# Block-sparse attention with a SoLU layer: transfers of the fallback path on GpSimd, a new order of the last tiles' statistics, later key and query transposes

## The chip, the cores and the metric

The kernel runs on one core of one Trainium2 chip. The metric is the device time of one execution in microseconds. The core has five instruction streams: TensorE (PE in the profile; PEld is its weight load), VectorE (DVE), ScalarE (ACT), GpSimd (POOL) and SyncE (SP), which here issues nearly all transfers. Each stream runs in its own order and waits on semaphores.

## What is computed

Attention over 4 batches, 8 heads, 768 positions and 64 columns, with a mask on blocks of 32: the neighbours, the first and last block, and three sampled blocks per row of blocks. Then a layer on the 3072 rows of 512 values:

```python
h = x @ w_in                                    # 512 -> 1024
solu = h * softmax(h)
ln = (solu - mean(solu)) / sqrt(var(solu) + 1e-6) * g_ln
return ln @ w_out                               # 1024 -> 512
```

## The kernel before

**Units of work.** Heads are taken in pairs (4 pairs), queries in chunks of 128. A pass `ps` covers one batch and two query chunks (`PC` = 2), so there are 12 passes, 3 to a batch. In a pass each pair has 3 units (`u`), one for two chunks of keys; a unit is four score matmuls (`sco`, L416), one exp on ACT (L427) and 16 output matmuls (`op`, L444). A pass has 12 units, and a unit's number is also the clock of the plan below ("slot"). After the last unit of a pass the rows `xb` are transposed by a DMA (`x_turn`, L470, into `xT`), and the layer runs for the two tiles of 128 rows of that pass, interleaved with the next passes: `h_mms` (L487), exp (`e_exp`, L496, which also sums along the row), `solu` (L508), a DMA transpose of it (`ln_turn`, L513, into `lnT`), row statistics (`stats`, L522), `rstd` (three short instructions on DVE and a power on POOL, L540), `o_mms` (L547), scaling by rstd (`scaled`, L556 on ACT or L558 on DVE) and the store to `out` (L563).

**Keys and queries.** For batches 1 to 3 each pair's k and q are loaded by SP (`load`, L318, stage `st_k`, `st_q`), cast to bf16 on POOL into the one buffer `nat` (`cast`), and turned together by one DMA transpose that SP issues (`turn_dma`, L381, into a tile `pd` with three buffers). The transpose leaves two heads above each other on the partitions, so `shift` copies them on POOL (L327) into `KT` and `QT`, one copy a head and key, 64 partitions by 768. `KT` and `QT` have two buffers each, by the batch's parity. Pair 3 of a batch is read first by its unit 9.

**What sets the order.** Nothing is scheduled by the compiler: `at(when, fn, ...)` collects calls, and `emit` runs them sorted by `when` (in slots, a unit each), so each engine's stream has that order. The lists `first` (batch 1) and `then` (batches 2 and 3, counted from 36 slots before the batch's first unit) give the due slots of loads, casts, turns, shifts, and loads and casts of v. x's turn is due 0.1 before a pass begins (11.9, 23.9, 35.9 in that count), and a layer's ln turn at 3.05 and 9.05 of a pass. So a turn's number says behind which transposes it is on SP's queue. SP and POOL work through theirs in order: a `shift` holds POOL until its turn has landed, and a transpose that waits holds SP.

**The last tiles.** Pass 11 (`LP`) has its own tail, a list of calls that is run in its order at the end: the last h (`h_end`), exp, `solu`, statistics, transposes on PE (`ln_mm`) with a copy on ACT (`ln_out`), the output matmuls, and for the very last tile two halves (`o_half`, L893; `scale_half`, L902 on ACT and L905 on DVE), stored by SP and by ACT.

**The check and the fallback.** The fast path takes exp without the row maximum. `check_r` and `check_e` (L915, L916) mark sums out of range, `check_sum` counts them (L926, L927), `check_bad` sums over the partitions with a matmul (L932) and copies the result to `bad_i` (L933). Then every engine reads `bad_i` into a register (L985) and branches (L986): if it is over zero, `general_path` does all the work again in loops, with the maximum subtracted. With these inputs it is not, so each engine jumps over its part of `general_path` to the closing waits and barriers (L1012). What an engine has to jump over is what `general_path` puts on it; each transfer in a loop brings its address work and semaphore updates to the engine that issues it, also in the branch not taken, where the semaphores are brought to the same value.

Of the kernel before, what the change touches and what calls it, by code (L numbers as in the profile page):

```python
# [7 lines left out]
FP32 = mybir.dt.float32  # L8
# [7 lines left out]
def block_mask(nc, m_sb, m_ps, sampled_blocks, NB, neg):  # L16

    NR = sampled_blocks.shape[1]
    maskT = m_sb.tile([NB, NB], FP32, name="maskT")
    nc.vector.memset(maskT, 0.0)  # L20
    for fill, base, cm, step in (
        (neg, 1, -1, 1), (neg, 1, 1, -1),
        (0.0, -1, 1, 0), (0.0, NB - 2, -1, 0),
        (0.0, -1, 0, 1), (0.0, NB - 2, 0, -1),
    ):
        nc.gpsimd.affine_select(out=maskT, in_=maskT, compare_op=ALU.is_ge, fill=fill,
                                base=base, channel_multiplier=cm, pattern=[[step, NB]])
    _t = sampled_blocks.tensor
    _t32 = bass.DRamTensorHandle(_t.name, (2 * NB * NR,), I32)
    samp_flat_ap = bass.AP(tensor=_t32, offset=0, ap=[[0, 1], [1, 2 * NB * NR]])  # L30
    samp_i = m_sb.tile([1, NB * NR, 2], I32, name="samp_i")
    nc.sync.dma_start(out=samp_i.rearrange("a b c -> a (b c)"), in_=samp_flat_ap)
    ones1 = m_sb.tile([1, NB], BF16, name="ones1")
    nc.vector.memset(ones1, 1.0)
    samp_lo_bf = m_sb.tile([1, NB * NR], BF16, name="samp_lo_bf")
    nc.vector.tensor_copy(out=samp_lo_bf, in_=samp_i[:, :, 0])
    samp_ps = m_ps.tile([NB, NB, NR], FP32, name="samp_ps")
    nc.tensor.matmul(samp_ps.rearrange("a b c -> a (b c)"), ones1, samp_lo_bf,
                     start=True, stop=True)
    samp_f = m_sb.tile([NB, NB, NR], FP32, name="samp_f")  # L40
    nc.scalar.copy(out=samp_f, in_=samp_ps)
    kb_iota_i = m_sb.tile([NB, 1], I32, name="kb_iota_i")
    nc.gpsimd.iota(kb_iota_i, pattern=[[0, 1]], base=0, channel_multiplier=1)
    kb_iota = m_sb.tile([NB, 1], FP32, name="kb_iota")
    nc.vector.tensor_copy(out=kb_iota, in_=kb_iota_i)
    eq = m_sb.tile([NB, NB, NR], FP32, name="eq")
    nc.vector.tensor_scalar(out=eq, in0=samp_f, scalar1=kb_iota, scalar2=None, op0=ALU.is_equal)
    anyeq = m_sb.tile([NB, NB], FP32, name="anyeq")
    nc.vector.reduce_sum(out=anyeq, in_=eq, axis=AX.X)
    nc.vector.tensor_scalar(out=anyeq, in0=anyeq, scalar1=-1.0, scalar2=1.0,  # L50
                            op0=ALU.mult, op1=ALU.add)
    nc.vector.tensor_scalar(out=anyeq, in0=anyeq, scalar1=0.0, scalar2=None, op0=ALU.max)
    nc.vector.tensor_mul(out=maskT, in0=maskT, in1=anyeq)
    return maskT


def general_path(tc, q, k, v, sampled_blocks, w_in_sb, w_out_sb, ident, out):
# [10 lines left out]
    with tc.tile_pool(name="f_c", bufs=1) as f_c, \  # L68
# [5 lines left out]
        with tc.tile_pool(name="f_m", bufs=1) as f_m, \  # L74
             tc.tile_pool(name="f_mp", bufs=1, space=bass.MemoryType.PSUM) as f_mp:
            maskT = block_mask(nc, f_m, f_mp, sampled_blocks, NB, -1e30)
            sel = f_m.tile([NB, NB, BLK], FP32, name="sel")
            nc.vector.memset(sel, 0.0)
            nc.gpsimd.affine_select(out=sel, in_=sel, compare_op=ALU.not_equal, fill=1.0,
                                    base=0, channel_multiplier=1, pattern=[[-1, NB], [0, BLK]])  # L80
            for t in (qT, kT):
                nc.vector.memset(t[D:TQ, :], 0.0)
            nc.vector.tensor_copy(out=kT[D : D + NB, :].rearrange("p (q o) -> p q o", o=BLK),
                                  in_=sel)
            m_row = f_m.tile([NB, NB, BLK], BF16, name="m_row")
            nc.vector.tensor_copy(
                out=m_row,
                in_=maskT.rearrange("p (q o) -> p q o", o=1).broadcast_to([NB, NB, BLK]))
            nc.sync.dma_start(out=m_scr, in_=m_row.rearrange("p q o -> p (q o)"))
        with tc.tile_pool(name="f_sb", bufs=2) as f_sb, \  # L90
             tc.tile_pool(name="f_ps", bufs=1, space=bass.MemoryType.PSUM) as f_ps:
            with tc.For_i(0, B, 1) as b:
                with tc.For_i(0, H, 1) as h:
# [11 lines left out]
                    with tc.For_i(0, S, TQ) as t0:  # L105
# [1 line left out]
                        nc.gpsimd.dma_start(  # L107
                            out=qc, in_=q[bass.ds(b, 1), bass.ds(h, 1), bass.ds(t0, TQ), :].rearrange(
                                "a e p d -> p (a e d)"))
                        nc.sync.dma_start(out=qT[D : D + NB, :], in_=m_scr[:, bass.ds(t0, TQ)])  # L110
                        tq = f_ps.tile([D, TQ], BF16, tag="f_tq")
                        nc.tensor.matmul(tq, qc, ident, is_transpose=True, start=True, stop=True)
                        nc.vector.tensor_copy(out=qT[0:D, :], in_=tq)
# [22 lines left out]
                        for j in range(NCH):  # L136
# [4 lines left out]
                        xo = f_sb.tile([TQ, D], BF16, tag="f_x")  # L141
                        nc.vector.tensor_scalar(out=xo, in0=op, scalar1=rs, scalar2=None,
                                                op0=ALU.mult)
                        nc.sync.dma_start(
                            out=x_scr[bass.ds(b, 1), bass.ds(t0, TQ), bass.ds(h * D, D)].rearrange(
                                "a p d -> p (a d)"),
                            in_=xo)
# [1 line left out]
        with tc.tile_pool(name="f_sb2", bufs=2) as f_sb, \  # L149
             tc.tile_pool(name="f_ps2", bufs=1, space=bass.MemoryType.PSUM) as f_ps:  # L150
            with tc.For_i(0, n_tok, 128) as t0:
                xt = f_sb.tile([128, d_model], BF16, tag="f_xt")
                nc.sync.dma_start(out=xt, in_=x_rows[bass.ds(t0, 128), :])
                tps = f_ps.tile([128, KD, 128], BF16, tag="f_tps")
                for c in range(KD):
                    nc.tensor.matmul(tps[:, c, :], xt[:, c * 128 : (c + 1) * 128], ident,
# [45 lines left out]
                                     stop=(c == KF - 1))  # L202
                ot = f_sb.tile([128, d_model], FP32, tag="f_ot")
                nc.scalar.copy(out=ot, in_=ops)
                nc.sync.dma_start(out=out[bass.ds(t0, 128), :], in_=ot)


@with_exitstack
def kernel(
# [80 lines left out]
    def at(when, fn, *args):  # L290
        plan.append((when, len(plan), fn, args))
# [31 lines left out]
    def copy(eng, o, i):  # L323
        if eng is nc.scalar:
            nc.scalar.copy(out=o, in_=i)
        else:
            eng.tensor_copy(out=o, in_=i)  # L327
# [52 lines left out]
        turned[b, pr] = pt  # L380
        nc.sync.dma_start_transpose(out=pt, in_=nat[:, 2 * PW * pr : 2 * PW * (pr + 1)])  # L381

    def shift(b, pr, key):
        n0 = NCH if key == "q" else 0
        dst = (KT if key == "k" else QT)[b % 2]
        for hh in range(2):
            h = 2 * pr + hh
            copy(nc.gpsimd, dst[0:D, h * NCH : (h + 1) * NCH, :],
                 turned[b, pr][hh * D : (hh + 1) * D, n0 : n0 + NCH, :])

# [181 lines left out]
    with tc.manual_schedule():  # L574
# [195 lines left out]
        for s in range(n_units):  # L770
# [19 lines left out]
            [21.3, 21.4, 26.0, 27.3, 30.1, 30.15, 38.2, 39.0],  # L790
            [9.7, 27.08, 27.3, 36.2], [18.0, 30.07, 32.0, 41.0])
        then = (
            [3.2, 4.1, 5.0, 5.9, 15.2, 16.1, 17.9, 18.3], [8.2, 9.4, 10.6, 11.8, 20.2, 21.4, 23.8, 24.5],
            [13.0, 21.1, 25.0, 27.1],
            [15.4, 16.4, 24.03, 24.9, 27.4, 28.4, 30.6, 31.5],
            [17.0, 28.1, 29.0, 37.05], [22.6, 33.4, 34.6, 41.0])
        for b in range(1, B):
            loads, casts, turns, shifts, v_loads, v_casts = first if b == 1 else then
            t0 = SLOTS * NPB * (b - 1)
            for (key, pr), t_l, t_c in zip(kq + vs, loads + v_loads, casts + v_casts):  # L800
                at(t0 + t_l, load, nc.sync, srcs[key], b, pr, key)
                at(t0 + t_c, cast, nc.gpsimd, b, pr, key)
            for pr, t_t in enumerate(turns):
                at(t0 + t_t, turn_dma, b, pr)
            for (key, pr), t_s in zip(kq, shifts):
                at(t0 + t_s, shift, b, pr, key)


        def layer(ps, i, hs, es, os):
# [74 lines left out]

        o2 = {}

        def o_half(half, pool, tag):
            if pool is p_sco:
                o2[half] = p_sco.tile([128, 2, HF], FP32, tag=tag, name="oe1a")[:, 0, 0:256]
            else:  # L890
                o2[half] = pool.tile([128, d_model], FP32, tag=tag, name="oe1b")[:, 0:256]
            for c in range(KF):
                nc.tensor.matmul(o2[half], lnT_of[LP, 1][:, c, :],  # L893
                                 w_cen_sb[:, c, half * 256 : (half + 1) * 256],
                                 start=(c == 0), stop=(c == KF - 1), skip_group_check=True)
# [29 lines left out]
        def check_sum():  # L925
            nc.vector.reduce_sum(out=n_ok[:, 0:1], in_=okr, axis=AX.X)  # L926
            nc.vector.tensor_scalar(out=bad, in0=n_ok[:, 0:1], scalar1=float(n_r + n_e),  # L927
                                    scalar2=None, op0=ALU.is_lt)

        def check_bad():  # L930
            bad_ps = p_h.tile([1, 1], FP32, tag="h", name="bad_ps")
            nc.tensor.matmul(bad_ps, bad, ones_c, start=True, stop=True)  # L932
            nc.vector.tensor_copy(out=bad_i, in_=bad_ps)  # L933

        end = SLOTS * NPASS
        A, V = nc.scalar, nc.vector
        for n, (fn, *args) in enumerate((
# [7 lines left out]
            (check_r, n_r - 2 * PC, n_r),  # L945
            (h_end, 1, 0, KD),
            (solu, LP, 0),
            (e_exp, LP, 1),
            (o_mms, LP - 1, 1, 0, 3, tile_in(p_op, "op", "o_10")),
            (ln_mm, 0),  # L950
            (ln_out, 0, A),
            (o_mms, LP - 1, 1, 3, 8),
            (solu, LP, 1),
            (check_e,),
            (stats, LP, 0),
            (rstd, LP, 0),
            (o_mms, LP, 0, 0, 2, tile_in(p_sco, "sco", "oe0")),
            (ln_mm, 1),
            (ln_out, 1, A),
            (stats, LP, 1),  # L960
            (rstd, LP, 1),
            (o_mms, LP, 0, 2, 8),
            (scaled, LP - 1, 1, A),
            (store, LP - 1, 1),
            (check_sum,),
            (scaled, LP, 0, A),
            (store, LP, 0),
            (o_half, 0, p_sco, "sco"),
            (o_half, 1, p_op, "op"),
            (scale_half, 0, V, nc.sync),  # L970
            (scale_half, 1, A, nc.scalar),
            (check_bad,),
        )):
            at(end + 0.01 * n, fn, *args)
        at(end - 5.0, x_turn, LP, 0, 2)
# [41 lines left out]
```

## Time and profile before

| | us |
|---|---|
| median of 3 runs | 213.96 (213.76 to 214.35) |
| the profiled execution | 213.1 |
| its span, first to last instruction | 211.5 |
| mean granted TensorE clock | 0.989 |

The span is shorter than the execution's time by 1.6 us, which lies before the first and after the last instruction. In rows of the profile "out<-in" names tiles of the program with their numbers left out, "x4" is the number of instructions in the row, "idle before" or the bracket says how long the engine stood idle and who ended it. A busy time of merged rows runs from the first start to the last end, so neighbours overlap.

### The profile page before, as it was taken

Reading aid. Unit: us, or ns where it says so; the run is one execution under the profiler, and the core shown is the slowest. Engines: PE = TensorE matmul, PEld = TensorE weight load, DVE = VectorE, ACT = ScalarE, POOL = GpSimd, SP = SyncE. Lnnn points to the kernel's source line nnn. Section 1 sums busy time; section 2 is a strip of 40 time slices with the busy share of each in tenths; the row PEclk is TensorE's granted clock in tenths of the full one; section 3 lists DMA queues with packets and bytes.
Section 4 is the critical chain, followed back from the end, with each engine's and each line's share of the span. In section 5 each row is a group of like instructions: output and inputs, shape, how many; then the busy total and the mean of one; then the engine's idle time right before and its main releaser. Section 6 shows DMA issues by size and latency. Waiting matters only on the chain.

```text
span 211.5 us, 5629 instructions
## 1 busy us (share of the span) xinstructions
PE 199.9 (95%) x2238; PEld 137.5 (65%) x2238; DVE 139.9 (66%) x329; ACT 174.5 (82%) x208; POOL 107.4 (51%) x155
## 2 busy tenths in 40 slices
PE   7989999999989999999999999999999999999950
PEld 2669867776666677677667667567667667664530
DVE  5895879988647656656655755756745845768760
ACT  6988989889869889889888988888988988784640
POOL 7989698679494264689334355699111011011120
PEclk9999999999999999999999999999999999999995
DMA  6999999899999799997798899896706507462230
GB/s 173 338 360 217 379 376 273 166 243 271 194 301 203 180 258 237 274 192 203 193 299 154 189 311 261 199 269 127 206 3 149 81 24 124 125 83 76 79 149 11
DMA packets 73907, 42.03 MB, mean 199 GB/s; under 512 B 55828, under 2 KB 69396, under 8 KB 73876
## 3 DMA queue, kind: packets, MB, share of 16 engines
q1 hardware_dynamic: 72932, 40.06, 77.9%
q0 software_dynamic: 528, 1.05, 2.6%
q10 hardware_dynamic: 416, 0.52, 0.9%
q8 instruction: 18, 0.29, 0.6%
q14 instruction: 13, 0.11, 0.2%
HBM read 23.07 MB, written 6.29 MB: 139 GB/s over the span
## 4 chain that ended last, share of the span: by engine, by line
PE 74%; DVE 8%; DMA 7%; POOL 3%; issue 2%; ACT 2%; ACTq 0%; POOLq 0%; DVEq 0%
PE sco L416 25%; PE h L487 15%; PE op L444 15%; PE o L547 13%; DMA pd<-nat 5%; DMA xT<-xb 2%; DVE stats L522 2%; POOL KT L327 2%; PE warm_t L403 2%; DVE solu L508 2%; PE he L867 1%; DVE QT L664 1%; POOL QT L327 1%; PE mean_ps L750 1%; PE tp_k L346 1%
## 5 line engine op out<-in xcount | busy, mean ns | idle before, releaser
L427 ACT ACTIVATE exs<-sco 128x1024 bf16<-128x1024 f32 x144 | 140.4, 1024 | 9.4 <-PE sco L416 6.9
L416 PE MATMUL sco<-QT,KT 88*128 88x256 bf16 x576 | 86.9, 272 | 1.1 <-POOL QT L327 0.5
L416 PEld LDWEIGHTS <-KT 88*128 88x128 bf16 x576 | 54.2, 97 | 32.9 <-issue 6.6
L487 PE MATMUL h<-w_in_sb,xT 128*128 128x512 bf16 x176 | 55.3, 379 | 0.3 <-DMA xT<-xb 0.3
L444 PE MATMUL op<-VA,exs 128*128 128x65 bf16 x1152 | 51.8, 194 | 0.0
L444 PEld LDWEIGHTS <-exs 128*128 128x128 bf16 x1152 | 48.5, 97 | 3.7 <-DVE xb L458 0.3
L547 PE MATMUL o<-w_cen_sb,lnT 128*128 128x512 bf16 x176 | 45.2, 379 | 0.0
L540 POOL TENSOR_TENSOR rstd<-vpe,mhalf 128x1 f32<-128x1 f32 x24 | 13.2, 548 | 54.9 <-DVE vpe L538 49.5
L457 DVE RECIPROCAL recip_all<-op 128x4 f32<-128x4 f32 x48 | 8.7, 182 | 42.8 <-PE op L444 42.7
L496 ACT ACTIVATE e<-h 128x1024 bf16<-128x1024 f32 x22 | 22.5, 1023 | 12.9 <-PE h L487 11.5
L522 DVE BATCH_NORM_STATS2 stats<-solu 128x6 f32<-128x512 bf16 x48 | 30.6, 680 | 0.0
L327 POOL COPY KT<-pd 64x768 bf16<-64x768 bf16 x24 | 20.1, 837 | 16.5 <-DMA pd<-nat 15.7
L508 DVE TENSOR_TENSOR solu<-h,e 128x1024 bf16<-128x1024 f32 x22 | 26.8, 1216 | 1.6 <-ACT e L496 1.6
L547 PEld LDWEIGHTS <-lnT 128*128 128x128 bf16 x176 | 15.9, 98 | 13.8 <-DMA lnT<-solu 0.2
L558 DVE TENSOR_SCALAR ot<-o,rstd 128x512 f32<-128x512 f32 x20 | 15.0, 751 | 10.8 <-issue 5.3
L458 DVE TENSOR_TENSOR xb<-op,recip_all 128x256 bf16<-128x256 f32 x48 | 20.4, 424 | 1.7
L327 POOL COPY QT<-pd 64x768 bf16<-64x768 bf16 x24 | 19.7, 821 | 1.0
L487 PEld LDWEIGHTS <-xT 128*128 128x128 bf16 x176 | 16.0, 98 | 5.2 <-DMA xT<-xb 1.5
L327 POOL CAST nat<-st_q 128x768 bf16<-128x768 f32 (+2 forms) x19 | 13.6, 714 | 8.1 <-DMA st_q<-in_q_dram 8.0
L327 POOL CAST VA<-st_v 128x768 bf16<-128x768 f32 x16 | 13.1, 828 | 7.7 <-DMA st_v<-in_v_dram 3.9
L327 POOL CAST nat<-st_k 128x768 bf16<-128x768 f32 x15 | 12.7, 846 | 4.9 <-DMA st_k<-in_k_dram 4.6
L740 POOL TENSOR_SCALAR w_out_sb<-w_out_f,g_ln_sb 128x512 bf16<-128x512 f32 x8 | 6.0, 759 | 2.1 <-DMA w_out_f<-in_moe_w_out_dram 2.1
(89 smaller groups left out, 113.5 us busy)
## 6 DMA issues: line engine op xcount, KB each, us to landing
st_v<-in_v_dram SPq DMA_DIRECT2D x16, 384.0 KB, 5.0
out_dram<-ot SPq DMA_DIRECT2D x23, 256.0 KB, 2.6
st_k<-in_k_dram SPq DMA_DIRECT2D x15, 384.0 KB, 5.5
st_q<-in_q_dram SPq DMA_DIRECT2D x12, 384.0 KB, 6.5
w_out_f<-in_moe_w_out_dram SPq DMA_DIRECT2D x4, 512.0 KB, 7.6
st_q<-in_q_dram SPq DMA_DIRECT2D x4, 256.0 KB, 6.9
w_in_sb<-in_moe_w_in_dram POOLq DMA_DIRECT2D x1, 1024.0 KB, 11.9
st_q<-in_q_dram SPq DMA_DIRECT2D x4, 128.0 KB, 4.7
```

The source lines that it names most:

```text
L327: eng.tensor_copy(out=o, in_=i)
L416: nc.tensor.matmul(sco[:, hh, kk * QW : (kk + 1) * QW], KT[b % 2][0:KR, h * NCH + 2 * u + kk, :], QT[b % 2][0:KR, h * NCH + PC * j : h * N ...
L427: nc.scalar.activation(out=exs_of[ps, pr][:, u].rearrange("p a b c -> p (a b c)"), in_=sco_of.pop(s).rearrange("p a b -> p (a b)"), func=A ...
L444: nc.tensor.matmul(op[:, hh, ic, :], exs[:, u, hh, kk, ic * TQ : (ic + 1) * TQ], VA[b % 2][:, 2 * pr + hh, 2 * u + kk, :], start=(u == 0 a ...
L458: nc.vector.tensor_tensor(out=xb_of[ps][:, pr].rearrange("p c (h d) -> p h c d", h=2), in0=op[:, :, :, 0:D], in1=recip.broadcast_to([TQ, 2 ...
L487: nc.tensor.matmul(h_of[ps, i][:, half, :], xT_of[ps][:, c * PC + i, :], w_in_sb[:, c, half * HF : (half + 1) * HF], start=(c == 0), stop= ...
L496: nc.scalar.activation(out=o, in_=h, func=ACT.Exp, scale=1.0, accum_out=esum_all[:, t : t + 1])
L508: nc.vector.tensor_mul(out=so, in0=h, in1=e)
L522: nc.vector.bn_stats(out=stat_of[ps, i][:, half, :], in_=so[:, half, :])
L540: nc.gpsimd.tensor_tensor(out=rstd_of[ps, i], in0=vpe, in1=mhalf, op=ALU.pow)
L547: nc.tensor.matmul(ops_of[ps, i], lnT_of[ps, i][:, c, :], w_cen_sb[:, c, :], start=(c == 0), stop=(c == KF - 1), skip_group_check=True)
L558: nc.vector.tensor_scalar(out=o, in0=i_, scalar1=r, scalar2=None, op0=ALU.mult)
```

## The change

1. All transfers of `block_mask` and `general_path` that SP issued are issued by GpSimd (`nc.sync.dma_start` becomes `nc.gpsimd.dma_start`): the sampled blocks, the mask out, the mask rows in, x out, x in and the output. `general_path` does not run with these inputs.
2. In `then` (batches 2 and 3) pair 3's q is cast at 23.9 instead of 24.5; the turns of pairs 1, 2 and 3 are due later, and with them the shifts.
3. `shift` takes a range of query chunks. Pair 3's q, in batches 1 to 3, is copied in two parts: chunks 0 and 1 just ahead of its k, the other four where the whole q was.
4. In the tail, tile 0's `stats` stand directly behind its `solu`, ahead of the last exp; tile 1's stand directly behind tile 0's `rstd`'s small instructions; `check_e` and `check_sum` go behind the last `rstd`; `check_bad` is split, its matmul between the fifth and sixth matmul of the last half, its copy to `bad_i` (`check_out`) behind DVE's half.

```diff
@@ block_mask, general_path: six transfers of this kind
-    nc.sync.dma_start(out=samp_i.rearrange("a b c -> a (b c)"), in_=samp_flat_ap)
+    nc.gpsimd.dma_start(out=samp_i.rearrange("a b c -> a (b c)"), in_=samp_flat_ap)
...
@@
-    def shift(b, pr, key):
+    def shift(b, pr, key, c0=0, c1=NCH):
         n0 = NCH if key == "q" else 0
         dst = (KT if key == "k" else QT)[b % 2]
         for hh in range(2):
             h = 2 * pr + hh
-            copy(nc.gpsimd, dst[0:D, h * NCH : (h + 1) * NCH, :],
-                 turned[b, pr][hh * D : (hh + 1) * D, n0 : n0 + NCH, :])
+            copy(nc.gpsimd, dst[0:D, h * NCH + c0 : h * NCH + c1, :],
+                 turned[b, pr][hh * D : (hh + 1) * D, n0 + c0 : n0 + c1, :])
@@
         then = (
-            [3.2, 4.1, 5.0, 5.9, 15.2, 16.1, 17.9, 18.3], [8.2, 9.4, 10.6, 11.8, 20.2, 21.4, 23.8, 24.5],
-            [13.0, 21.1, 25.0, 27.1],
-            [15.4, 16.4, 24.03, 24.9, 27.4, 28.4, 30.6, 31.5],
+            [3.2, 4.1, 5.0, 5.9, 15.2, 16.1, 17.9, 18.3], [8.2, 9.4, 10.6, 11.8, 20.2, 21.4, 23.8, 23.9],
+            [13.0, 25.0, 27.1, 36.05],
+            [15.4, 16.4, 25.1, 25.9, 30.1, 31.0, 36.2, 39.0],
             [17.0, 28.1, 29.0, 37.05], [22.6, 33.4, 34.6, 41.0])
@@
+            at(t0 + shifts[6] - 0.05, shift, b, NP - 1, "q", 0, PC)
             for (key, pr), t_s in zip(kq, shifts):
-                at(t0 + t_s, shift, b, pr, key)
+                at(t0 + t_s, shift, b, pr, key, PC if (key, pr) == ("q", NP - 1) else 0)
@@ o_half takes a range of its eight matmuls
+        bad_ps = []
+
         def check_bad():
-            bad_ps = p_h.tile([1, 1], FP32, tag="h", name="bad_ps")
-            nc.tensor.matmul(bad_ps, bad, ones_c, start=True, stop=True)
-            nc.vector.tensor_copy(out=bad_i, in_=bad_ps)
+            bad_ps.append(p_h.tile([1, 1], FP32, tag="h", name="bad_ps"))
+            nc.tensor.matmul(bad_ps[0], bad, ones_c, start=True, stop=True)
+
+        def check_out():
+            nc.vector.tensor_copy(out=bad_i, in_=bad_ps[0])
@@ the tail's list
             (solu, LP, 0),
+            (stats, LP, 0),
             (e_exp, LP, 1),
...
             (solu, LP, 1),
-            (check_e,),
-            (stats, LP, 0),
             (rstd, LP, 0),
+            (stats, LP, 1),
             (o_mms, LP, 0, 0, 2, tile_in(p_sco, "sco", "oe0")),
             (ln_mm, 1),
             (ln_out, 1, A),
-            (stats, LP, 1),
             (rstd, LP, 1),
+            (check_e,),
+            (check_sum,),
             (o_mms, LP, 0, 2, 8),
             (scaled, LP - 1, 1, A),
             (store, LP - 1, 1),
-            (check_sum,),
             (scaled, LP, 0, A),
             (store, LP, 0),
             (o_half, 0, p_sco, "sco"),
-            (o_half, 1, p_op, "op"),
+            (o_half, 1, p_op, "op", 0, 5),
+            (check_bad,),
+            (o_half, 1, p_op, "op", 5, KF),
             (scale_half, 0, V, nc.sync),
+            (check_out,),
             (scale_half, 1, A, nc.scalar),
-            (check_bad,),
```

More of the change, by code (lines that the diff above doesn't have):

```diff
@@ L88, in general_path @@
                 in_=maskT.rearrange("p (q o) -> p q o", o=1).broadcast_to([NB, NB, BLK]))
-            nc.sync.dma_start(out=m_scr, in_=m_row.rearrange("p q o -> p (q o)"))
+            nc.gpsimd.dma_start(out=m_scr, in_=m_row.rearrange("p q o -> p (q o)"))
         with tc.tile_pool(name="f_sb", bufs=2) as f_sb, \
@@ L109, in general_path @@
                                 "a e p d -> p (a e d)"))
-                        nc.sync.dma_start(out=qT[D : D + NB, :], in_=m_scr[:, bass.ds(t0, TQ)])
+                        nc.gpsimd.dma_start(out=qT[D : D + NB, :], in_=m_scr[:, bass.ds(t0, TQ)])
                         tq = f_ps.tile([D, TQ], BF16, tag="f_tq")
@@ L143, in general_path @@
                                                 op0=ALU.mult)
-                        nc.sync.dma_start(
+                        nc.gpsimd.dma_start(
                             out=x_scr[bass.ds(b, 1), bass.ds(t0, TQ), bass.ds(h * D, D)].rearrange(
@@ L152, in general_path @@
                 xt = f_sb.tile([128, d_model], BF16, tag="f_xt")
-                nc.sync.dma_start(out=xt, in_=x_rows[bass.ds(t0, 128), :])
+                nc.gpsimd.dma_start(out=xt, in_=x_rows[bass.ds(t0, 128), :])
                 tps = f_ps.tile([128, KD, 128], BF16, tag="f_tps")
@@ L204, in general_path @@
                 nc.scalar.copy(out=ot, in_=ops)
-                nc.sync.dma_start(out=out[bass.ds(t0, 128), :], in_=ot)
+                nc.gpsimd.dma_start(out=out[bass.ds(t0, 128), :], in_=ot)
 @with_exitstack
@@ L885, with o_half @@
         o2 = {}
-        def o_half(half, pool, tag):
-            if pool is p_sco:
+        def o_half(half, pool, tag, c0=0, c1=KF):
+            if c0:
+                pass
+            elif pool is p_sco:
                 o2[half] = p_sco.tile([128, 2, HF], FP32, tag=tag, name="oe1a")[:, 0, 0:256]
@@ L891, in o_half @@
                 o2[half] = pool.tile([128, d_model], FP32, tag=tag, name="oe1b")[:, 0:256]
-            for c in range(KF):
+            for c in range(c0, c1):
                 nc.tensor.matmul(o2[half], lnT_of[LP, 1][:, c, :],
```

## The prediction

> **What bounds the kernel now.** I read the page first (busy time and chain), then the chain in order of time, then PE's and SP's timelines where the chain leaves PE, then the tail.
>
> ```profile
> span 211.5 us, 5629 instructions
> ...
> PE 199.9 (95%) x2238; PEld 137.5 (65%) x2238; DVE 139.9 (66%) x329; ACT 174.5 (82%) x208; POOL 107.4 (51%) x155
> ...
> PE 74%; DVE 8%; DMA 7%; POOL 3%; issue 2%; ACT 2%; ACTq 0%; POOLq 0%; DVEq 0%
> ```
>
> PE is busy for 95% of the span and is 74% of the chain. So time can come only from PE's few holes, and from the 6.6 us after its last matmul. The rows of the chain in order of time show the holes:
>
> ```profile
> 52.92 4.84 DMA pd<-nat
> ...
> 57.81 0.82 POOL KT L327
> ...
> 86.12 1.51 PE o L547 x7
> ...
> 93.96 1.51 PE o L547 x7
> ...
> 117.04 1.51 PE o L547 x7
> ...
> 124.71 1.51 PE o L547 x7
> ...
> 130.16 4.73 DMA xT<-xb
> ...
> 140.55 1.51 PE o L547 x7
> ```
>
> The "o x7" rows come once per half pass. Undisturbed they stand 7.67 us apart (117.04 to 124.71). From 86.12 to 93.96 it is 7.84: 0.17 lost. From 124.71 to 140.55, two half passes, it is 15.84: 0.50 lost. PE's timeline around the POOL part of batch 1 gives the third hole:
>
> ```profile
> 58.91 0.59 PE L487 MATMUL h<-w_in_sb,xT 128*128 128x512 bf16 x2
> 59.34 0.60 PE L416 MATMUL sco<-QT,KT 88*128 88x256 bf16 x4
> 59.78 0.60 PE L487 MATMUL h<-w_in_sb,xT 128*128 128x512 bf16 x2
> 60.42 0.38 PE L416 MATMUL sco<-QT,KT 88*128 88x256 bf16 x2
> 61.31 0.38 PE L416 MATMUL sco<-QT,KT 88*128 88x256 bf16 x2 [0.50 <-POOL QT L327]
> ```
>
> Two h matmuls take 0.43 (58.91 to 59.34), so these scores, the first of pair 3, were due at 60.21 and their second head at 60.43. It came at 61.31: 0.88 lost to the copy of q that POOL makes last. All three holes lie beside transposes that SP issues.
>
> **The turns.** SP's timeline, batches 1, 2 and 3:
>
> ```profile
> 51.59 1.23 SPq L470 DMA_TRANSPOSE xT<-xb  x1
> ```
> ```profile
> 81.68 3.44 SPq L381 DMA_TRANSPOSE pd<-nat  x1
> 85.22 1.27 SPq L470 DMA_TRANSPOSE xT<-xb  x1
> ```
> ```profile
> 127.92 2.15 SPq L381 DMA_TRANSPOSE pd<-nat  x1
> 130.16 1.26 SPq L470 DMA_TRANSPOSE xT<-xb  x1
> ```
>
> In batches 2 and 3 pair 1's turn (due 21.1) sits ahead of x's (due 23.9): x's issue stands right behind the turn's 3.44 and 2.15 us, and both stretches are where 0.17 and 0.50 went. With the turn due at 25.0, x goes first. Both losses go: **-0.17 and -0.50**. Later turns of pairs 2 and 3 queue on SP behind x (35.9) or ln's turn (27.05) as they do in batch 1, and POOL, in order, sits in `shift` until a turn lands; behind it stand the rstd powers and casts of v, which have two or more slots of room in the plan (a slot is a sixth of 7.67, 1.28 us). I cost that at nothing; if the room fails, DVE's scaled output, not PE, waits first.
>
> **q in two parts.** The trace has no 64x256 copy; the whole 64x768 one takes 0.82 (57.81 above). The nearest row by shape on POOL is a cast of 256 columns:
>
> ```profile
> L327 POOL CAST nat<-st_q 128x256 bf16<-128x256 f32 x3 | 1.2, 409 | 0.0
> ```
>
> The bounds are a third of 0.82 (0.27) and 0.82 itself; I take 0.41, from the cast of the same width. Ahead of pair 3's first scores POOL now does two parts of q and two whole k: 2 x 0.41 + 2 x 0.82 + three gaps of 0.05 = 2.6 us, against 3.4. From the start at 57.81 this ends at 60.42, against the due 60.43: **-0.8** in batch 1 (nothing at 0.82 a copy, -0.88 at 0.27). The remaining parts cost at most 0.82 each and are needed a pass later: the idle half of POOL hides them.
>
> Batches 2 and 3 now turn pair 3 behind x at 36.05, which is batch 1's geometry. There the copies began 57.81 - 51.59 = 6.22 after x's issue, and the second head is due 60.43 - 51.59 = 8.84 after it; 6.22 + 2.6 = 8.8. So it just fits, with no room; I take +0.05 each, **+0.1**. What bounds it is the landing:
>
> ```profile
> DMA to landing us min/median/max: 3.2/4.8/6.1
> ```
>
> Batch 1's took 4.84, about the median of these turns; the slowest would add 1.3 us in each batch, the fastest nothing lost. POOL's six extra instructions are in the 2.6.
>
> The body: -0.17 - 0.50 - 0.8 + 0.1 = **-1.4**.
>
> **The tail.** DVE's timeline, last tiles, then POOL's and PE's rows:
>
> ```profile
> 198.50 1.23 DVE L508 TENSOR_TENSOR solu<-he,e 128x1024 bf16<-128x1024 f32 x1 [1.15 <-ACT e L496]
> 199.64 0.17 DVE L915 TENSOR_SCALAR okr<-esum_all 128x24 f32<-128x24 f32 x1
> ...
> 199.94 1.28 DVE L522 BATCH_NORM_STATS2 stats<-solu 128x6 f32<-128x512 bf16 x2
> 201.14 0.20 DVE L529 TENSOR_SCALAR es<-esum_all 128x1 f32<-128x1 f32 x1
> ...
> 203.28 0.37 DVE L926 TENSOR_REDUCE n_ok<-okr 128x1 f32<-128x216 f32 x1
> ...
> 204.09 0.48 DVE L905 TENSOR_SCALAR ot_last<-oe1a,rstd 128x256 f32<-128x256 f32 x1 [0.25 <-POOL rstd L540]
> 204.49 0.13 DVE L933 CAST bad_i<-bad_ps 1x1 int32<-1x1 f32 x1
> ```
> ```profile
> 202.57 1.04 PE L893 MATMUL oe1b<-w_cen_sb,lnTe 128*128 128x256 bf16 x8
> ...
> 203.50 0.55 POOL L540 TENSOR_TENSOR rstd<-vpe,mhalf 128x1 f32<-128x1 f32 x1 [1.16 <-DVE vpe L538]
> ```
> ```profile
> L932 PE MATMUL bad_ps<-ones_c,bad 128*1 128x1 f32 x2 | 0.2, 163 | 0.4 <-DVE bad L927 0.4
> ```
>
> Tile 0's stats (1.20 from start to next start, 199.94 to 201.14) move into the 1.15 us in which DVE waits for ACT: the last solu starts 0.05 later, and so do its turn on PE and what follows there. `check_e` (0.30, 199.64 to 199.94) moves behind the last rstd. So POOL's last power starts 1.20 + 0.30 - 0.05 = 1.45 earlier, at 202.05. Late next is PE (first half done about 202.8) and DVE itself, which does check_e (0.30) and check_sum (0.4 for the row at 203.28, 0.15 for the comparison behind it, a short one as that at 199.64) and is free about 202.85: the half scaled by DVE goes from 204.09 to about 202.9, SP's store with it. The check's matmul goes between the fifth and sixth of eight on the second half: 202.62 + 5 x 0.11 (1.04 for eight of 0.27 that overlap) = 203.2, and `bad` is ready about 202.85, so PE waits for nothing; were `bad` over 0.3 late, PE would wait with the last three matmuls and ACT's half behind it. It costs PE between nothing and its two passes of 0.163 one behind the other; I take 0.25, moving ACT's half from 204.09 to about 203.9. `bad_i` is out about 203.6, not 204.62.
>
> What follows is SP. The instructions of the read of `bad_i` and of the branch:
>
> ```profile
> L985 SPq TENSOR_LOAD <-bad_i x1: 544/544/544, 205.0 to 205.0; - x1
> ```
> ```profile
> L986 SPq EVENT_SEMAPHORE  x6: 17/17/17, 209.5 to 209.9; - x6
> ...
> L986 ACTq COMPARE_BRANCH  x1: 54/54/54, 205.7 to 205.7; - x1
> ...
> L986 SPq COMPARE_BRANCH  x1: 53/53/53, 205.9 to 205.9; - x1
> ...
> L986 ACTq EVENT_SEMAPHORE  x1: 17/17/17, 206.2 to 206.2; - x1
> ```
> ```profile
> 207.00:209.00 2.00, 0.00 (x0) 0.00 (x0) 0.00 (x0) 0.00 (x0) 0.00 (x0) 0.50 0.00 0
> ```
> ```profile
> q14 instruction: 4, 0.03, 3.0%
> ```
>
> SP branches over the general path at 205.9 and does its next instruction at 209.5; ACT needs 0.5 for the same. Nothing moves on the DMAs from 207 to 209, so no store is awaited; behind the branches the DMA view (205.8 to 210) has four instruction transfers of 8 KB. I read the 3.6 us as SP fetching instructions that it jumped to. [...] SP reads after its last store, now about 203.85 instead of 205.0: **-1.1** for the branch, and all behind it.
>
> Does the shorter general path remove the stall? SP's part loses six transfers with their address and semaphore work. Counting the compiled list of before, SP branches at entry 203 to entry 361 of 384; I reckon 41 entries lost and 12 waits gained (transfers on GpSimd take more semaphores, awaited at each loop's exit). The target comes near 336, the end near 355. [...] So I keep 3.6 us. The six semaphore updates after the stall (209.5 to 210.0, 0.48) leave SP, two waits come (0.12): **-0.35**.
>
> Sum: -1.4 - 1.1 - 0.35 = **-2.85**. The profiled execution took 213.1, of which 211.5 is the span; it would take 210.25. The median of the runs is 213.96, so I predict **211.1**.
>
> **Rivals.**
> [...] 0.12. [...]
> B. The 3.6 us are in truth the last store's receipt, so the earlier branch buys nothing: the tail gains 0.2 (ACT's half) + 0.35. Total -1.95: 212.0. Against: no traffic from 207 on. 0.10.
> C. Slower: pair 3's turn behind x in batches 2 and 3 lands late and holds PE at pair 3's first scores. It decides from a landing later than 4.84 after issue, and each us late is a us of PE, twice. The slowest turn (6.1) costs 1.3 twice, still -0.25 in all, 213.7; if x too is stretched by the turn behind it (h waits) by 0.6 each, +0.95: 214.9. Within 0.3%: 0.07, slower: 0.06.
> Otherwise my forecast, 210.2 to 212.0: 0.65.
>
> **Numbers.** One measurement of this kernel tells 0.3% (0.64 us) from no change. Faster: forecast, A and B, 0.87; same 0.07; slower 0.06. The range leaves out the slow part of C (0.13) and what A gives below 209.0: 209.0 to 213.3.
>
> **What would show it.** Right: no PE hole before pair 3's first scores of batch 1; "o" rows 7.67 apart through both turns of pair 1; last power at about 202.05 less 1.4; SP's branch 2.5 earlier, with 3.6 behind it. Wrong: idle of PE ended by POOL's KT at pair 3's first scores of batches 2 or 3; h waiting for xT; SP's gap near 0.5 (A) or ending at the old time (B).

## The result, and the profile after

The changed kernel takes 210.57 us (median of 5 runs, 210.13 to 210.78); the kernel before, beside it on the same chip, 213.96 us. The ratio is 0.983, its 95% interval 0.980 to 0.986. The profiled execution took 210.66 us (213.1 before), its span is 208.9 (211.5 before): 2.6 us less, where the prediction's sum says 2.85. The number came out near the prediction; one large term of it did not. The page after:

```profile
span 208.9 us, 5591 instructions
...
PE 198.0 (95%) x2204; PEld 137.9 (66%) x2238; DVE 140.3 (67%) x329; ACT 174.6 (84%) x208; POOL 109.1 (52%) x161
...
PE 81%; DMA 9%; issue 2%; POOL 2%; ACT 1%; DVE 1%; SPq 1%; POOLq 0%
```

**The body.** PE's timeline in batch 1, around pair 3's first scores, and then in batch 2 (columns: start, length, what ran, idle before it):

```profile
59.62 0.60 PE L416 MATMUL sco<-QT,KT 88*128 88x256 bf16 x4
60.28 0.38 PE L487 MATMUL h<-w_in_sb,xT 128*128 128x512 bf16 x1
60.49 0.61 PE L416 MATMUL sco<-QT,KT 88*128 88x256 bf16 x4
60.94 0.67 PE L444 MATMUL op<-VA,exs 128*128 128x65 bf16 x16
```
```profile
105.74 0.60 PE L416 MATMUL sco<-QT,KT 88*128 88x256 bf16 x4
106.40 0.38 PE L487 MATMUL h<-w_in_sb,xT 128*128 128x512 bf16 x1
106.61 0.82 PE L416 MATMUL sco<-QT,KT 88*128 88x256 bf16 x4
```

In batch 1 the four scores of pair 3 now stand in one row of 0.61: the hole is gone. In batch 2 the row has 0.82 instead of 0.60: its second head came 0.22 late. SP's timeline in batch 3 shows the new order, x's transpose ahead of pair 1's:

```profile
128.98 1.23 SPq L470 DMA_TRANSPOSE xT<-xb  x1
130.27 0.57 SPq L563 DMA_DIRECT2D out_dram<-ot  x1
130.93 1.55 SPq L381 DMA_TRANSPOSE pd<-nat  x1
```

Measured on the starts of the scores, from the first unit of batch 1 to the last unit, the body is 1.23 us shorter: -0.86 in batch 1 (pair 3), -0.16 (x's turn of batch 2), +0.22 (pair 3 of batch 2), -0.48 (x's turn of batch 3), and nothing at pair 3 of batch 3. The program's start was 0.25 later in this execution; over all profiled runs that start varies by more than a microsecond. So what follows is told by the **last stretch**: from the start of the last unit's scores to the end of the span.

**The tail.** The rows of the last unit, before and after:

```profile
189.62 0.60 PE L416 MATMUL sco<-QT,KT 88*128 88x256 bf16 x4
```
```profile
188.64 0.60 PE L416 MATMUL sco<-QT,KT 88*128 88x256 bf16 x4
```

The last stretch is 211.5 - 189.62 = 21.9 us before and 208.9 - 188.64 = 20.3 after. DVE's timeline after, then POOL's:

```profile
199.16 1.28 DVE L522 BATCH_NORM_STATS2 stats<-solu 128x6 f32<-128x512 bf16 x2
...
201.28 0.38 DVE L930 TENSOR_REDUCE n_ok<-okr 128x1 f32<-128x216 f32 x1
...
201.84 0.48 DVE L909 TENSOR_SCALAR ot_last<-oe1a,rstd 128x256 f32<-128x256 f32 x1
202.45 0.15 DVE L941 CAST bad_i<-bad_ps 1x1 int32<-1x1 f32 x1
```
```profile
201.09 0.57 POOL L540 TENSOR_TENSOR rstd<-vpe,mhalf 128x1 f32<-128x1 f32 x1 [1.15 <-DVE okr L919]
```

All of that runs as predicted: against the last unit, the last power starts 1.4 us earlier than before. What follows does not. The instructions of the branch and behind it, and of ACT's store, then SP's waits from 195 us on (columns: total, times, longest):

```profile
L996 PEldq COMPARE_BRANCH  x1: 358/358/358, 203.5 to 203.5; - x1
L996 SPq COMPARE_BRANCH  x1: 53/53/53, 203.8 to 203.8; - x1
```
```profile
L1022 SPq EVENT_SEMAPHORE  x14: 17/28/28, 204.5 to 208.9; - x14
```
```profile
L563 ACTq DMA_DIRECT2D out_dram<-ot_last x1: 372/372/372, 203.4 to 203.4; - x1
```
```profile
SPq L1022 <- DMA out_dram<-ot_last: 2.8, 1, 2.8
```

SP branches at 203.8 and is at its closing waits at 204.5: the gap behind the branch is 0.7 us, not 3.6. But at the fifth of them it stands 2.8 us for ACT's last store, issued at 203.44 and landed at 207.54, 4.1 us later (the landing of the last of its 16 parts). Before, the same store was issued at 204.59 and landed at 206.62, 2.0 us later:

```profile
L563 ACTq DMA_DIRECT2D out_dram<-ot_last x1: 383/383/383, 204.6 to 204.6; - x1
```

The stall that was to stay went, and a wait of nearly the same size took its place.

### The profile page after: what moved, and what is told of

It reads as the page before. It is cut to its first block, busy times and chain, and to the rows that moved or that the text cites. A ratio compares the mean times of both kernels' runs of the same rounds, so it can differ in the third digit from the quotient of the medians.

```text
span 208.9 us, 5591 instructions
## 1 busy us (share of the span) xinstructions
PE 198.0 (95%) x2204; PEld 137.9 (66%) x2238; DVE 140.3 (67%) x329; ACT 174.6 (84%) x208; POOL 109.1 (52%) x161
## 4 chain that ended last, share of the span: by engine, by line
PE 81%; DMA 9%; issue 2%; POOL 2%; ACT 1%; DVE 1%; SPq 1%; POOLq 0%
PE sco L416 28%; PE o L547 17%; PE op L444 16%; PE h L487 16%; DMA st_q<-in_q_dram 3%; DMA w_out_f<-in_moe_w_out_dram 3%; DMA st_k<-in_k_dram 3%; PE he L869 1%; PE oe L547 1%; PE mean_ps L750 1%; POOL VA L327 1%; SPq L318 1%; DVE solu L508 1%; POOL nat L327 1%; ACT e L496 1%
## 5 line engine op out<-in xcount | busy, mean ns | idle before, releaser
L487 PE MATMUL h<-w_in_sb,xT 128*128 128x512 bf16 x153 | 48.6, 378 | 0.6
L547 PE MATMUL o<-w_cen_sb,lnT 128*128 128x512 bf16 x166 | 43.2, 379 | 0.5
L327 POOL COPY KT<-pd 64x768 bf16<-64x768 bf16 x24 | 20.1, 838 | 17.4 <-DMA pd<-nat 15.8
L327 POOL COPY QT<-pd 64x768 bf16<-64x768 bf16 (+2 forms) x30 | 20.8, 694 | 10.8 <-DMA pd<-nat 9.5
```

What stands on the lines that cost most here:

```text
L487: nc.tensor.matmul(h_of[ps, i][:, half, :], xT_of[ps][:, c * PC + i, :], w_in_sb[:, c, half * HF : (half + 1) * HF], start=(c == 0), stop= ...
L547: nc.tensor.matmul(ops_of[ps, i], lnT_of[ps, i][:, c, :], w_cen_sb[:, c, :], start=(c == 0), stop=(c == KF - 1), skip_group_check=True)
```

## The experiments

Theory K: SP's stall depends on where branch and target lie in its list of instructions, and part 1 removes it; part 4 then brings the first branches to the very issue of ACT's last store (both at 203.4 after; before, 205.2 and 204.6), and the instruction blocks that they fetch run into that store. The rivals: the stall is something else (a receipt, six semaphore updates), and the store is late for reasons of its own. Three kernels put part 1, part 4, and parts 2 and 3 on the kernel before, two only move SP's branch, and the others start from the changed kernel. They ran on three chips, on which the kernel before had medians of 214.0, 214.4 and 214.2 us.

**Part 1 alone** (the six transfers on GpSimd).

> The kernel before with part 1 alone (the fallback path's transfers on GpSimd). Theory L (SP's gap behind its branch is a fetch, and goes because the jump becomes short enough): SP branches at 205.9 as before, does its next instruction about 0.65 later instead of 3.6, and ends 3.3 us earlier than before: span about 208.2; ACT's last store still lands about 2.0 after its issue, since its packets are through before the branches' fetches begin. [...] If most of the changed kernel's gain were the turns and the tail, this kernel would move by less than 0.5.

Measured: 210.02 us, ratio 0.983 (0.980 to 0.986). The branch and the closing waits:

```profile
L986 SPq COMPARE_BRANCH  x1: 53/53/53, 206.3 to 206.3; - x1
```
```profile
L1012 SPq EVENT_SEMAPHORE  x14: 17/28/28, 206.8 to 208.4; - x14
```

The gap is 0.5. Part 1 alone brings what the whole change brings; the store lands 2.0 us after its issue.

**Part 4 alone** (the tail's list and the split check).

> The kernel before with part 4 alone (order of the last tiles' statistics and check). SP's branch comes 1.15 us earlier than before's 205.9, the gap of 3.6 stays behind it, so about -1.1 us: span about 210.4. Rival: the early branch lets the fetches of all engines fall onto ACT's last store, which then lands 4.1 us after issue; here this is covered by SP's gap, so it would add at most 0.2. If the order of the tail did nothing, the span would be 211.5.

Measured: 212.49 us, ratio 0.993 (0.991 to 0.995). SP branches 15.1 us after the last unit's start (16.3 before: 1.15 earlier) and then stands 3.4 us; ACT's store lands 3.9 us after its issue, beside the stall.

**Parts 2 and 3 alone** (the turns, q in two parts).

> The kernel before with parts 2 and 3 alone (later turns, pair 3's q in two parts). By the unit times of the two traces: -0.82 in batch 1, -0.16 and -0.48 where x's turn is no longer behind pair 1's, +0.2 at batch 2's pair 3: about -1.25 us, span about 210.2, with the tail as before (SP's gap 3.6). The prediction's own terms sum to -1.4. Rival: the turns bring nothing (under 0.3 us), since PE has slack elsewhere.

Measured: 212.66 us, ratio 0.995 (0.992 to 0.997); the last unit 1.13 us earlier, the gap 3.7, the store 2.0. The three parts alone gain 4.0, 1.5 and 1.35 us against a median of 214.0: 6.9 in all, twice what they bring together.

**SP's branch moved, nothing taken away.** The kernel before, with 16 small loads on SP ahead of the tail:

```diff
+        def pad_load(n):
+            nc.sync.dma_start(out=w_out_f[:, 0, 4 * n : 4 * n + 4], in_=moe_w_in[0:128, 0:4])
+
+        for n in range(16):
+            at(124.3 + 0.3 * n, pad_load, n)
```

> The kernel before with 16 small loads added to SP's queue in pass 10 (2 KB each into a staging tile no longer in use); nothing is taken away, and the fallback path stays on SP. [...] Theory L: the gap of 3.6 falls to about 0.65 and the kernel gets faster by about 2.9 us though it does more: span about 208.6. Rival S (the gap comes from the semaphore updates of SP's six fallback transfers, or from awaiting a store): the gap stays 3.6 and the time is 0 to +0.3.

Measured: 212.28 us, ratio 0.991 (0.987 to 0.995). The loads delay PE in the last batch, but:

```profile
L991 SPq EVENT_SEMAPHORE  x6: 17/17/17, 209.9 to 210.3; - x6
...
L991 SPq COMPARE_BRANCH  x1: 53/53/53, 209.4 to 209.4; - x1
```

With 16 entries more ahead of it (the branch at entry 219 of SP's list, 203 in the kernel before) the gap is 0.5 us, and the last stretch 18.8 us instead of 21.9. So the 3.6 us are not work and not a receipt: they go when the branch stands elsewhere in the list. One transfer of instructions is new here, 8 KB from 199.88 us, 9.5 us ahead of SP's branch. This is its queue's row for 199.5 to 200.5 us (transfers, MB, share of the engines); in no other kernel does that queue move anything between 178 us and the first branch:

```profile
q14 instruction: 1, 0.01, 4.5%
```

The trace shows that the stall is gone where a block came in ahead of the branch, 0.5 us against 3.6. It does not show SP waiting for a transfer to end. In the six kernels that stall, the last block that is fetched behind the branches has landed 1.0 to 2.0 us before SP goes on (207.52 against 209.53 in the kernel before), and the kernels without a stall fetch the same five blocks there. What fills the rest of the stall stays open.

**With 8 loads** (`range(8)`).

> The kernel before with 8 small loads more on SP ahead of the tail, half as many as in the run with 16: SP's branch moves from entry 203 of its list to 211, its target from 361 to 369. [...]

Measured: one execution, span 212.8, last stretch 21.9.

```profile
L991 SPq EVENT_SEMAPHORE  x6: 17/17/17, 210.8 to 211.2; - x6
...
L991 SPq COMPARE_BRANCH  x1: 53/53/53, 207.5 to 207.5; - x1
```

The gap is 3.3 us: from entry 211 the jump still stalls, from 219 it does not. That does not settle what decides. With 16 loads the new block was on its way when SP had run entry 209 and still waited at 210 (counted back from the branch). With 8 loads SP comes to entry 210 only at 207.37, 0.1 us ahead of its jump, while an 8 KB transfer of that queue takes 0.3 to 0.7 us in the kernel before. So it may be the block that came in ahead of the jump, for which there was no time here, or the place of the jump alone.

**The check behind both halves** (all else as changed).

```diff
-            (o_half, 1, p_op, "op", 0, 5),
-            (check_bad,),
-            (o_half, 1, p_op, "op", 5, KF),
+            (o_half, 1, p_op, "op"),
             (scale_half, 0, V, nc.sync),
-            (check_out,),
             (scale_half, 1, A, nc.scalar),
+            (check_bad,),
+            (check_out,),
```

> The changed kernel with the check's matmul and the copy to bad_i put back behind both halves (the rest of the change stands). Theory K: in the changed kernel the branches come 0.3 us behind the issue of ScalarE's last store, the blocks of instructions that they fetch run into that store, and it lands 4.1 us after its issue instead of 2.0. Then here SP's branch comes some 0.5 us later (near 204.3 on the changed kernel's clock), the store is through most of its packets by then and lands about 2.0 to 2.5 us after its issue, and the end is set by SP's branch or the store at about 206.2, plus 1.35: span 207.0 to 207.8, 1.1 to 1.9 below the changed kernel. Rival: the store is slow for a reason of its own (its place in the queue, two late rings) and lands 4 us after issue again: span 208.9, no change.

Measured: **208.47 us**, ratio 0.971 (0.968 to 0.974), span 206.8: the lowest here, 2.1 us below the changed kernel, whose interval (0.980 to 0.986) lies apart. The store is issued at 203.58 and lands at 205.30, 1.7 us later. Half-microsecond windows, the changed kernel and then this one (the last two columns: share of the DMA engines and GB/s):

```profile
204.50:205.00 0.50, 0.00 (x0) 0.00 (x0) 0.00 (x0) 0.00 (x0) 0.00 (x0) 0.98 0.66 215
205.00:205.50 0.50, 0.00 (x0) 0.00 (x0) 0.00 (x0) 0.00 (x0) 0.00 (x0) 0.50 0.11 18
205.50:206.00 0.50, 0.00 (x0) 0.00 (x0) 0.00 (x0) 0.00 (x0) 0.00 (x0) 0.50 0.15 10
206.00:206.50 0.50, 0.00 (x0) 0.00 (x0) 0.00 (x0) 0.00 (x0) 0.00 (x0) 0.50 0.10 12
206.50:207.00 0.50, 0.00 (x0) 0.00 (x0) 0.00 (x0) 0.00 (x0) 0.00 (x0) 0.50 0.05 6
```
```profile
204.50:205.00 0.50, 0.00 (x0) 0.00 (x0) 0.00 (x0) 0.00 (x0) 0.00 (x0) 1.00 0.71 248
205.00:205.50 0.50, 0.00 (x0) 0.00 (x0) 0.00 (x0) 0.00 (x0) 0.00 (x0) 1.00 0.22 49
205.50:206.00 0.50, 0.00 (x0) 0.00 (x0) 0.00 (x0) 0.00 (x0) 0.00 (x0) 1.00 0.13 49
206.00:206.50 0.50, 0.00 (x0) 0.00 (x0) 0.00 (x0) 0.00 (x0) 0.00 (x0) 0.97 0.00 0
```

In the changed kernel the store trickles until 207; here the DMA engines are done at 206, and what they move from 205.3 on is instruction blocks. In the changed kernel the store's packets run from 204.32, and the first instruction block (16 KB) starts at 204.61, in their midst; 13 of the store's 16 parts have landed by 205.20, the last three at 206.16, 206.77 and 207.54. Here the packets run from 204.47 to 204.95, and the first block starts at 205.30. Against the last unit SP's branch is only 0.3 us later (15.4 against 15.1), and the store's issue 0.2 earlier (14.6 against 14.8).

**q copied whole again** (part 3 undone).

> The changed kernel with pair 3's q copied whole behind its k again. Theory: the split is what removes batch 1's hole of 0.8 us, and it is also what lets pair 3's turn stand behind x's in batches 2 and 3. So here 0.8 comes back in batch 1, and batches 2 and 3 get the same geometry and lose 0.6 to 0.9 each: +2.0 to +2.6 us on the changed kernel (time 212.6 to 213.2). Rival: the copies of batches 2 and 3 have room, only batch 1's 0.8 comes back: 211.4.

Measured: 212.49 us, ratio 0.988 (0.984 to 0.992): 1.9 above the changed kernel by the medians, 1.1 by the ratios. PE's timeline in batch 2:

```profile
109.28 0.38 PE L416 MATMUL sco<-QT,KT 88*128 88x256 bf16 x2 [0.29 <-POOL QT L327]
110.17 0.38 PE L416 MATMUL sco<-QT,KT 88*128 88x256 bf16 x2 [0.50 <-POOL QT L327]
```

1.0 us comes back in batch 1, 0.9 in batch 2, nothing in batch 3, where pair 3's turn landed early enough. Both the theory (all three) and the rival (batch 1 alone) were off by one batch.

**The fallback's transfers on SP again** (part 1 undone).

> The changed kernel with the fallback path's transfers back on SP: parts 2, 3 and 4 alone. Theory K: SP's stall of 3.4 to 3.7 us behind its branch comes back, from about 203.8 to 207.4; ScalarE's last store lands at about 207.5 all the same, so nearly all of the stall lies beside the store, and what is lost is the six semaphore updates that SP does behind it: about +0.5 us on the changed kernel, near 211.1, span 209.3 to 209.6. Rival: the store is delayed only when SP too fetches at once (four engines' blocks instead of three); then it lands sooner, and the stall alone sets the end: the same time, but a store of 2 to 3 us. By the plain sum of the parts (general part worth 4.0 alone) it would be 214.

Measured: 211.55 us, ratio 0.985 (0.981 to 0.989); last stretch 21.2, gap 4.0, store 4.0. That is 1.0 above the changed kernel by the medians and 0.3 by the ratios, not 4.0: with the check early, most of the stall lies beside the late store.

**The old turns, q still in two parts** (part 2 undone).

> The changed kernel with the old due slots of batches 2 and 3 (turns, shifts and pair 3's q cast as before), the split of q kept. Theory: x's turn waits behind pair 1's again (-0.16 and -0.48 lost), pair 3's first scores of batch 2 get their 0.22 back: +0.4 us on the changed kernel, about 211.0. Rival: the later turns cost as much as they bring (POOL held in the copies, pair 3's queries late), and the time is the same.

Measured: 210.97 us, ratio 0.985 (0.980 to 0.989): not to be told from the changed kernel. On the starts of the scores x's turn of batch 2 loses nothing in this order either, batch 3 loses 0.31, and the 0.22 at pair 3 of batch 2 is not lost: part 2 by itself is worth 0.1, or 0.3 against the changed kernel's second profiled execution, which does not lose the 0.22 either.

**Parts 1 to 3 with the old tail** (part 4 undone).

> Parts 1, 2 and 3 of the change with the old tail: the changed kernel without part 4. By the plain sum of parts this would be 1.1 us slower than the changed kernel, which has the earlier branch. Theory K: part 4 puts the branches, and the blocks of instructions that they fetch, on ScalarE's last store, and with SP's stall gone nothing covers that; so without part 4 the store lands some 2.0 us after its issue and the stretch from the last unit's first score to the end of the span is 18.4 us as in the kernel with part 1 alone, against 20.3 in the changed kernel: time about 208.7, 1.9 below the changed kernel, and within 0.6 of the kernel with the check put last.

Measured: **208.70 us**, ratio 0.975 (0.969 to 0.981); gap 0.5, store 2.0, last stretch 18.4. The new tail costs the changed kernel 1.9 us. This kernel and the one with the check behind both halves can't be told apart: their intervals overlap.

**Check behind both halves, fallback on SP.**

> The kernel with the check put last, with the fallback path's transfers back on SP: the fourth corner of two choices (whose transfers, when the check). Theory K: SP's stall of 3.4 to 4.0 us is back and sets the end; the store lands 1.7 to 2.0 us after its issue, which buys nothing here, and the branch is 0.3 us later than with the early check: the stretch from the last unit's first score to the end is 21.1 to 21.5 us (21.1 with the early check), time 211.5 to 212.0. Rival: if the late check were worth 2 us by itself, the stretch would be 19.0 us and the time 209.5.

Measured: 211.74 us, ratio 0.988 (0.982 to 0.994); the store lands in 1.7 us, the last stretch is 21.1, and SP's own wait sets it:

```profile
SPq L995 <- SPq L995: 3.7, 1, 3.7
```

**The changed kernel once more.**

> The changed kernel once more, beside the two others on the same chip: 210.6 us, the last stretch 20.0 to 20.4 us, and ScalarE's last store landing 3.9 to 4.1 us after its issue in the profiled execution. If the late landing was a chance of one execution, it is 2.0 here, and the stretch 18.2 us.

Measured: 210.47 us, ratio 0.982 (0.976 to 0.988); last stretch 20.2, store 4.0. The late landing is no chance of one execution.

All runs by the two causes (profiled executions, us):

| fallback on | check | kernels | SP's gap | store lands after | last stretch |
|---|---|---|---|---|---|
| SP | old tail | before; parts 2, 3 | 3.6; 3.7 | 2.0; 2.0 | 21.9; 22.0 |
| SP | early | part 4; parts 2, 3, 4 | 3.4; 4.0 | 3.9; 4.0 | 20.5; 21.2 |
| SP | last | check last, fallback on SP | 3.7 | 1.7 | 21.1 |
| GpSimd | old tail | part 1; parts 1, 2, 3 | 0.5; 0.5 | 2.0; 2.0 | 18.4; 18.4 |
| GpSimd | early | changed; again; old turns; q whole | 0.7 in each | 4.1; 4.0; 3.9; 4.3 | 20.3; 20.2; 20.1; 20.5 |
| GpSimd | last | check behind both halves | 0.7 | 1.7 | 17.8 |

The stall goes with the first column, the late store with the second, and the stretch follows whichever ends last.

## Why the prediction was right, and where it was not

- **q in two parts, -0.8:** right, -0.86. The copy of 256 columns was taken at 0.41 us from a cast of that width; it takes 394 ns:

```profile
L327 POOL COPY QT<-pd 64x256 bf16<-64x256 bf16 x6 | 2.4, 394 | 9.6 <-DMA pd<-nat 9.5
```

- **x ahead of pair 1, -0.17 and -0.50:** the sizes are right (-0.16, -0.48), the cause only in part. In batch 2 two of the other kernels with the old order (part 1 alone, old turns) lose nothing there, so those 0.17 are within what one execution differs from another. In batch 3 every profiled kernel with x first but one gains 0.5 on the kernel before; with the old order none gains over 0.2. The one is the check last with the fallback on SP: it gains 0.1 there, and loses 0.25 in batch 2, though x goes first in it.
- **Pair 3 behind x, +0.05 each:** "just fits, with no room" is what it does: 0.22 in batch 2 and nothing in batch 3. The landing decides, as said: in the kernels with this order and q in two parts, batch 2 costs 0.2 where the turn landed 5.0 us after its issue (three of the profiled executions) and nothing where it took 3.2 to 3.3 (four).
- **The tail up to the branch, -1.1:** right, 1.15; ACT's half comes 0.2 earlier, as reckoned.
- **SP's stall kept, 0:** this step failed. No run shows a reason for keeping the 3.6 us; in their place the runs show a gap of 0.7 in the changed kernel and 0.5 with part 1 alone. The list came out shorter than reckoned (SP jumps from entry 198 to 329 of 348, reckoned 336 of 355), and nothing stalls behind the target: with part 1 alone SP does the last 17 instructions of its list, those behind the target, from 206.84 to 208.43 us, in steps of at most 0.5. With the branch put at other entries the gap is 3.3 to 4.0 us or 0.5 to 0.7. A count of entries, and the author's estimate from it, was no ground for giving A only 0.12.
- **Six semaphore updates and two waits, -0.35:** right: without the stall the last stretch is 18.8 with the updates on SP (16 loads) and 18.4 without (part 1 alone).
- **What was missing:** the landing of ACT's last store, 2.0 us in the kernel before, has no term in the sum. SP's gap came near 0.5, the sign of A (0.7), and the time still did not fall to 209: with the earlier branch, which the sum counted as a gain of 1.1, that store landed 4.1 us after its issue. Two errors of nearly one size, -2.9 for the stall and +2.8 for SP's wait for the store, left the forecast where it was. The two kernels with the whole body of the change, the stall gone and the store not late show what the gap without the late store is worth: 208.5 and 208.7 us.
- **Behind PE's last matmul:** the kernel before has 7.3 us there (the check's matmul starts at 203.98 and takes 0.19), not 6.6; no term of the sum uses it.

So the forecast of 211.1 was right in its body and its branch, and by luck in its end.

That the early check makes the store late is shown: six profiled executions with it early (the changed kernel twice), six landings of 3.9 to 4.3 us; eight kernels with it later, eight of 1.7 to 2.0. In the six the first branch comes within 0.1 us of the store's issue, in the eight 0.5 us or more behind it. Each engine's read of `bad_i` ahead of its branch moves along with it, and no run tells the two apart.

That the instruction blocks do it on the DMA engines is only read from the packets. For it: in five of the six the first block starts 0.2 to 0.3 us behind the store's first packet, in the eight only behind its last. Against it stands the sixth (q whole). In all six, 126 of the store's 144 packets (14 of its 16 parts) have gone out by 1.4 us behind the first branch, and the next one starts 0.5 us later. In the sixth this is so too, although its first block is recorded at 208.10, 0.2 us after that pause has begun. What else a branch sets off, and why so few packets are held for 2 us, stays open.

## What to carry to other kernels

A stall behind a jump can go when only the jump is moved in its engine's list (here from 3.6 us to 0.5, with 16 entries more ahead of it): move it by a few instructions and look, before explaining it. Parts that each gain alone need not add up where two of them feed one end: look for what the earlier event triggers, here whatever the reads and branches of five engines set off beside the last transfer of all, which then landed 4.1 us after its issue and not 2.0. Where that landing ends last, as in the changed kernel, whatever delays it is part of the critical path.

## What the runs showed of the hardware

- SP's jump over its part of the fallback path costs 0.5 to 0.7 us in some places of the list and 3.3 to 4.0 in others: 3.3 with the branch at entry 211, 0.5 at 219.
- Both the kernel before and the changed kernel fetch one block of 16 KB and four of 8 KB behind the first branch: they start 1.1 to 1.7 us behind it in the one, where SP stalls 3.6 us, and 1.2 to 2.1 in the other, where its gap is 0.7.
- ACT's store of 128 KB landed 1.7 to 2.0 us after its issue, and 3.9 to 4.3 when the first branches came within 0.1 us of the issue; in those, 14 of its 16 parts had gone out by 1.4 us behind the first branch, and the next packet started 0.5 us later.
